# An attention and feed-forward kernel on one core: the list schedule's durations, its transfers, its buffers and its order made anew

## The chip, the core and the metric

The kernel runs on one core of one Trainium2 chip. The metric is the device time of one execution in microseconds (us). A core has five engines with an instruction queue each, and each works through its queue in order: PE (TensorE, matrix products; its weight loads are shown apart as PEld), DVE (VectorE), ACT (ScalarE), POOL (GpSimd) and SP (SyncE), which here only issues transfers (DMAs). An engine that waits for a semaphore holds up all that stands behind the waiting instruction in its queue.

## What is computed

Attention over 8 sequences of 576 positions with 8 heads of 64, a causal window of 128 and a linear bias; its output is the input of a feed-forward layer of 2048 hidden units without biases. All of it is float32.

```python
# attention: q, k, v are [8, 8, 576, 64]
scores = scale * np.matmul(q, k.transpose(0, 1, 3, 2))
mask = (rel >= 0) & (rel < window)                     # rel = row - column, window = 128
scores = np.where(mask, scores + bias[None], -1000000000.0)
attn = np.exp(scores - np.max(scores, axis=-1, keepdims=True))
attn = attn / (np.sum(attn, axis=-1, keepdims=True) + 1e-09)
x = np.matmul(attn, v)                                 # then [4608, 512]
# feed-forward: w_in [512, 2048], w_out [2048, 512]
h = x @ w_in
g = h * erf(np.maximum(h, 0.0) + np.log1p(np.exp(-np.abs(h))))
out = g @ w_out
```

## The kernel before

**Stages.** The 4608 tokens are cut into 12 chunks of 384 (`CH`). A unit of attention is one chunk and one pair of heads, 48 units u in all, four to a chunk. For each of a unit's three tiles PE computes the scores s (L408, float32), DVE adds the bias and finds the row's extreme (L415, two instructions and two short reads of the accumulator), ACT takes the exponential in place in p (L425), DVE inverts the sums (L438 and L439), POOL scales p (L448). PE then transposes p into t (L466), ACT or DVE copies t to pT (L348 or L350), PE multiplies by v into px (L499), and px is split into a rounded part (a copy by ACT or DVE, L348 or L350) and a remainder (DVE, L509), both in the chunk's tile x. Every feed-forward product is made of three float32r products of such parts.

**Two passes.** The first pass (`first_pass`) computes the hidden units of the first 6 of 16 weight blocks as soon as a chunk's x is there: h (L706, per chunk and block two groups of six matmuls of 384 columns), a copy to hs, softplus and erf on ACT in batches (L737 to L740, with table loads), a product and a split on DVE and ACT (L748, L689 or L691, L753), and the products o with w_out (L769, 512 columns). Its partial sums go to DRAM (`pd`, L783). Each x is saved to DRAM as well (`xd`, L681). The second pass (`second_pass`) does the other ten blocks on pairs of chunks with fewer products (`pair`: the tiles pa, pb, pc, L908; copies of pa by `snap` at L689 or L691, sums by `add` at L919), then the same activation (L949, L951) and the products po, pxt, ps, pt (L979); the partial sums are added at L791 and stored at L796. Its weights are prepared in small portions while attention runs (`spare_pair`, `spare_out`: loads `wri` and `wro` at L533, DVE and ACT instructions at L541 to L595, stores `wd` at L600 and L629) and fetched back later.

**What sets the order.** No queue is written by hand. All instructions are registered with `Plan.op`, with an estimated duration on each engine that could take them, the tiles they read and write, and a due time `at`. `Plan.run` (L155) is a list scheduler: it steps through an imagined time, and on each engine starts the ready operation with the lowest due time whose tiles find a free place (`fits`, L198); an operation that ACT or DVE can do goes to the one that is free. The order in which operations start there is the order in which they are emitted into the queues. Durations (`dve`, `act`, `fp32_us`, `f32r_us`, `dma`, L273 to L290), the delay from an engine to the next (`hop`), the moment when a tile's place comes free and the landing of transfers are guesses: on the chip each queue keeps the planned order, but instructions wait for what they really depend on.

**Places.** Tiles live in rings whose sizes are the constants at the top: `NKB` places for q and k, `NQ` for v, `PB` for p, `TB` for pT, `XB` (4) for x, `MB` (18) for the hidden tiles, two each for the staging tiles of weights. PSUM has one bank each for s, t and px and two for h and the second pass' pa, pb, pc. In the first `SPARE` units the scores also use the h banks and the transposes also an o bank. In the first `SINGLE` units each tile's sums are inverted alone, later three together. `NSV` chunks hold their saves of x back until the chunk's last h (L684 and L710). 40 short products on a zero tile (`warm_up`, L343) have the latest due time and fill PE where nothing else is ready.

```python
if c < NSV:
    self.held.setdefault(c, []).append(o)
```

## Time and profile before

| | |
|---|---|
| median of 3 runs | 1035.49 us (1035.35 to 1036.95) |
| the profiled execution's own time | 1035.51 us |
| its span, from the first to the last instruction | 1033.5 us |
| PE busy in the span | 1015.7 us (98%) |
| DVE, ACT, POOL busy | 659.5, 639.8, 161.1 us |
| mean granted TensorE clock | 0.998 |
| moved by DMA | 190.98 MB |

A profile's row names the line, the engine, the operation and the tiles (out<-in, buffer numbers left out), then how often it occurs; a group's row gives the busy time in us, the mean of one in ns, and the idle time of the engine just before it with what ended it. A row of the timeline has the start and the length in us and, in square brackets, the idle time before it and what ended it. A matmul's end is modelled: of matmuls in a row the starts tell the pace, not the lengths.

### The profile page before, as it was taken

The numbers are of one execution on the slowest core, as the hardware profiler recorded it, in microseconds if no ns is written. First come the engines' busy times: TensorE is split into PE (matmuls) and PEld (weight loads), VectorE is DVE, ScalarE is ACT, GpSimd is POOL, SyncE is SP. The second block draws the span as 40 slices with busy tenths as digits, with TensorE's granted clock in tenths as the row PEclk, the third lists the DMA queues.
The fourth block names the chain that finished last, engine by engine and source line by source line (L and its number), as shares of the span: only waits on it lengthen the run. The fifth ranks groups of instructions, "written<-read, shape, count | busy, mean of one in ns | idle before, by whom it ended". The sixth has DMA issues, their size and how long they took to land.

```text
span 1033.5 us, 16056 instructions
## 1 busy us (share of the span) xinstructions
PE 1015.7 (98%) x5612; PEld 927.4 (90%) x5612; DVE 659.5 (64%) x1565; ACT 639.8 (62%) x1283; POOL 161.1 (16%) x294
## 2 busy tenths in 40 slices
PE   9899999989999999999999999999999999999998
PEld 8799998988899899998999998998998988989986
DVE  5888886867788868455347456556566566565532
ACT  5678775766677777666557655645545546548460
POOL 2634234323432213411000000000000000000000
PEclk9999999999999999999999999999999999999999
DMA  9775468689779785563787423324324314310302
GB/s 366 277 250 190 140 205 307 229 287 306 266 297 337 249 300 191 195 226 130 274 326 260 147 96 129 113 87 135 115 75 140 122 66 149 123 62 31 119 4 72
DMA packets 63760, 190.98 MB, mean 185 GB/s; under 512 B 7104, under 2 KB 7872, under 8 KB 63680
## 3 DMA queue, kind: packets, MB, share of 16 engines
q1 hardware_dynamic: 62992, 189.43, 53.1%
q8 instruction: 45, 0.74, 0.3%
q10 hardware_dynamic: 688, 0.52, 0.2%
q14 instruction: 35, 0.29, 0.1%
HBM read 137.76 MB, written 52.17 MB: 184 GB/s over the span
## 4 chain that ended last, share of the span: by engine, by line
PE 87%; DMA 8%; DVE 2%; ACT 1%; issue 1%; POOL 1%; SPq 0%; POOLq 0%; DVEq 0%; ACTq 0%
PE o L769 12%; PE h L706 12%; PE pa L908 12%; PE po L979 12%; PE px L499 8%; PE s L408 7%; PE pc L908 6%; PE pt L979 4%; PE ps L979 4%; PE pxt L979 4%; PE t L466 3%; PE pb L908 3%; DMA xd<-x 2%; DMA qk<-qk_a 1%; DMA wri<-w_in 1%
## 5 line engine op out<-in xcount | busy, mean ns | idle before, releaser
L448 POOL TENSOR_SCALAR p<-p,st 128x192 f32<-128x192 f32 (+1 forms) x288 | 160.4, 575 | 310.5 <-DVE st L439 187.7
L706 PE MATMUL h<-x,wi 128*128 128x384 f32 x864 | 178.3, 347 | 0.5 <-DVE st L438 0.5
L706 PEld LDWEIGHTS h<-x,wi 128*128 128x128 f32 x864 | 150.1, 188 | 3.6 <-PE s L408 0.8
L769 PE MATMUL o<-wo,gh 128*128 128x512 f32 x432 | 144.3, 415 | 0.0
L425 ACT ACTIVATE p<-p,st 128x192 f32<-128x192 f32 (+1 forms) x288 | 124.7, 436 | 19.9 <-DVE st L415 19.6
L689 ACT COPY hs<-pa 128x384 f32<-128x384 f32 x82 | 39.2, 478 | 133.0 <-PE pa L908 132.9
L408 PE MATMUL s<-qk 128*128 128x192 f32 (+1 forms) x576 | 111.5, 318 | 3.9 <-DVE st L415 2.9
L908 PE MATMUL pa<-t,p 128*128 128x384 f32 x540 | 109.3, 337 | 0.2 <-DVE hs L691 0.2
L499 PE MATMUL px<-pT,v 128*128 128x192 f32 (+2 forms) x704 | 105.4, 298 | 2.4 <-DVE x L509 2.0
L499 PEld LDWEIGHTS px<-pT,v 128*128 128x128 f32 x704 | 102.1, 193 | 6.0 <-DVE x L509 2.9
L908 PEld LDWEIGHTS pa<-t,p 128*128 128x128 f32 x540 | 96.4, 188 | 6.4 <-DVE hs L691 0.6
L408 PEld LDWEIGHTS s<-qk 128*128 128x128 f32 x576 | 90.7, 191 | 8.1 <-DVE st L415 2.2
L979 PE MATMUL po<-ho,gh 128*128 128x512 f32 x270 | 90.7, 390 | 0.0
L689 ACT CAST gh<-hs 128x768 fp32r<-128x768 f32 x66 | 55.0, 837 | 56.0 <-DVE hs L959 49.7
L415 DVE CUSTOM_DVE_ANT_0 p<-s,bias 128x192 f32<-128x192 f32 x224 | 70.9, 354 | 26.9 <-PE s L408 20.1
L769 PE MATMUL o<-wo,gl 128*128 128x512 f32 x216 | 85.4, 395 | 0.0
L769 PEld LDWEIGHTS o<-wo,gh 128*128 128x128 f32 x432 | 76.2, 189 | 7.7
L466 PE MATMUL t<-ident,p 128*128 128x128 f32 x400 | 67.7, 275 | 5.6 <-POOL p L448 3.1
L979 PE MATMUL po<-ho,gl 128*128 128x512 f32 x180 | 70.8, 394 | 0.0
L348 ACT COPY pT<-t 128x384 f32<-128x384 f32 (+1 forms) x81 | 36.5, 454 | 49.8 <-PE t L466 45.6
L466 PEld LDWEIGHTS t<-ident,p 128*128 128x128 f32 x400 | 49.6, 144 | 19.1 <-POOL p L448 7.1
L959 DVE TENSOR_TENSOR hs<-s,hs 128x768 f32<-128x768 f32 x60 | 55.4, 952 | 17.0 <-ACT s L951 17.0
(276 smaller groups left out, 1830.0 us busy)
## 6 DMA issues: line engine op xcount, KB each, us to landing
qk<-qk_a SPq DMA_DIRECT2D x31, 768.0 KB, 5.9
xd<-x SPq DMA_DIRECT2D x24, 768.0 KB, 7.1
qk<-qk_c SPq DMA_DIRECT2D x16, 960.0 KB, 6.2
v<-v_a SPq DMA_DIRECT2D x32, 384.0 KB, 5.0
v<-v_c SPq DMA_DIRECT2D x16, 640.0 KB, 4.8
pd<-ot SPq DMA_DIRECT2D x36, 256.0 KB, 4.9
out<-pd SPq DMA_DIRECT2D x36, 256.0 KB, 3.0
p<-wd SPq DMA_DIRECT2D x35, 256.0 KB, 5.1
```

The source lines that it names most:

```text
L408: nc.tensor.matmul(ps[:, j, :n], lhsT=q(t, j), rhs=k(j, off, n), start=True, stop=True)
L415: nc.vector.tensor_tensor_reduce(out=pt[:, c0:, j, :], in0=ps[:, j, :n].rearrange("p (c d) -> p c d", d=D), in1=self.bias[g][:, j, 0::3] i ...
L425: nc.scalar.activation(dst, dst, AF.Exp, bias=low[t][:, j : j + 1], scale=-1.0, accum_out=sums[t][:, j : j + 1])
L448: nc.gpsimd.tensor_scalar(dst, dst, sums[t][:, j : j + 1], 1.0, op0=ALU.mult, op1=ALU.mult)
L466: nc.tensor.matmul(two[:, :, (2 - cb) * D : (3 - cb) * D], lhsT=p[t][:, cb].rearrange("p j d -> p (j d)"), rhs=self.ident[:, :], is_transp ...
L499: nc.tensor.matmul(px[:, to : to + m * D], lhsT=v[:, blk].rearrange("p j d -> p (j d)"), rhs=run(src, m, 256)[:, :, :D], start=first and x ...
L689: self.nc.scalar.copy(out, src)
L706: nc.tensor.matmul(ps[:, :CH], lhsT=ww[:, cs], rhs=xx[:, k], start=(k2 + k + n == 0), stop=(k2 + k + n == 4),)
L769: nc.tensor.matmul(po.all, lhsT=g[:, j, cs], rhs=w.all, start=(u["start"] and n == 0), stop=(u["end"] and n == 2),)
L908: nc.tensor.matmul(dst[:, :CH], lhsT=wv[i](k), rhs=xb[l][:, k], start=start and k + n == 0, stop=k + n == 3, skip_group_check=not start)
L959: op({"DVE": dve(2 * CH)}, lambda e, s=s, hs=hs: V.tensor_tensor(hs.all, s.all, hs.all, ALU.mult), r=[s, *parts], w=parts, at=at)
L979: nc.tensor.matmul(po.all, lhsT=g[:, k, cs], rhs=w.all, start=start and n == 0, stop=end and n == 2)
```

## The change

The scheduler's guesses are replaced. (1) Durations: the fixed part of a VectorE operation falls from 0.14 to 0.047 us, that of a ScalarE one from 0.17 to 0.088 (0.053 out of PSUM), a GpSimd scaling's from 0.49 to 0.24; short float32 matmuls are given twice the time they had. (2) Transfers: before, transfers run one after the other in the plan and an issue behind eight in flight is made longer; now those in flight share the bandwidth by the sizes of their packets (`land`), with 1.3 us (loads) or 0.9 us (stores) after the data, and with eight in flight SP does not issue another one. (3) A tile's place is free in the plan only some 0.1 to 0.2 us after its last user's end (`rest`), and `hop` adds a `tail` for some operations. (4) A GpSimd operation does not start in the plan while a VectorE operation marked `port` runs; GpSimd is asked before VectorE. (5) Constants: `NQ` 3 to 2, `PB` 6 to 9, `TB` 2 to 3, `KH` 4 to 2, `SPARE` 6 to 5, `SINGLE` 2 to 4, `NSV` 5 to 2; the due times of attention (`TE`, `NE`), of the activation (`MC`), of the second pass' products (`MP` 24 to 16) and of the weights (`W1R`; `WS`, `WSD`: the portions of the second pass' weights begin at 110 instead of 140 and are 19 instead of 11 apart). No computation changes; line numbers in the changed kernel are 48 higher from `Attention` on.

```diff
...
-SPARE = 6
-SINGLE = 2
+SPARE = 5
+SINGLE = 4
 WARM = 40
 
-MB, KH, KS = 18, 4, 3
-NQ, NKB, PB, XB, OB, TB = 3, 2, 6, 4, 5, 2
-
-TE, NE = 5.0, 6
+MB, KH, KS = 18, 2, 3
+NQ, NKB, PB, XB, OB, TB = 2, 2, 9, 4, 5, 3
+
+TE, NE = 4.5, 10
 TA = 6.5
-LL, LN, LT = 22, 0.3, 1
+LL, LN, LT = 22, 1, 1
 LEAD = 45
...
-MC, MP, MH = 4, 24, -16
+MC, MP, MH = 0.01, 16, -16
...
-WS, WSD, NWH = 140, 11, 2
-W1R, NSV, GSV = 12, 5, 5
+WS, WSD, NWH = 110, 19, 2
+W1R, NSV, GSV = 8, 2, 5
...
-    def hop(self, src, dst):
+    def hop(self, o, dst):
+        src = o.engine
         if src == "PE":
-            return 0.0 if "PE" in dst else 0.2
-        return 0.2 if "Pool" in dst else 0.14
+            return 0.0 if "PE" in dst else 0.21
+        if o.moved:
+            return 0.14
+        return o.tail + (0.12 if src == "Pool" else 0.28 if "Pool" in dst else 0.15)
 
     def __init__(self):
         self.ops = []
         self.slots = {}
 
-    def op(self, costs, emit, r=(), w=(), at=0.0, moved=0, rows=1.0, count=0):
+    def op(self, costs, emit, r=(), w=(), at=0.0, moved=0, packet=0.0, after=0.0, rows=1.0, count=0, tail=0.0, port=False):
         o = Op()
-        o.count = count
+        o.count, o.tail, o.packet, o.after, o.port, o.landed = count, tail, packet, after, port, False
...
-        transfer, flight = 0.0, []
+        flows, queued, issued, shared = [], [], [], 0.0
+        clock = 0.0
+        used = []
...
+        def land(t):
+
+            nonlocal clock
+            while True:
+                begin = queued[0][0] if queued else 1e9
+                whole = sum(f[1] for f in flows)
+                least = min(flows, key=lambda f: f[0] / f[1]) if flows else None
+                end = clock + least[0] * whole / least[1] if flows else 1e9
+                to = min(begin, end, t)
+                for f in flows:
+                    f[0] -= (to - clock) * f[1] / whole
+                clock = to
+                if end <= to + 1e-9:
+                    flows.remove(least)
+                    o = least[2]
+                    o.lag = clock + o.after - o.end
+                    heapq.heappush(done, (clock + o.after, o.seq, o))
+                    heapq.heappush(events, clock + o.after)
+                elif begin <= to + 1e-9:
+                    o = queued.pop(0)[1]
+                    flows.append([o.moved, o.packet * o.count, o])
+                else:
+                    break
+            nxt = min(begin, end)
+            if nxt < 1e9:
+                heapq.heappush(events, nxt)
+
+        def rest(o):
+            return o.tail + {"PE": 0.21, "SP": 0.14, "Pool": 0.12}.get(o.engine, 0.15)
+
         def fits(o):
+            if o.count and not all(x.landed for x in issued[: max(0, len(issued) + o.count - 8)]):
+                return False
...
-            while done and done[0][0] <= t + 1e-9:
-                _, _, o = heapq.heappop(done)
+            land(t)
+            while used and used[0][0] <= t + 1e-9:
+                _, _, o = heapq.heappop(used)
                 for b in o.bufs:
                     b.users -= 1
                     if b.users == 0 and b.tag is not None:
                         empty[key(b)].append(b.slot)
+            while done and done[0][0] <= t + 1e-9:
+                _, _, o = heapq.heappop(done)
+                o.landed = True
+                while issued and issued[0].landed:
+                    issued.pop(0)
+                over = o.end + o.lag + rest(o)
+                heapq.heappush(used, (over, o.seq, o))
+                heapq.heappush(events, over)
                 for x in o.outs:
                     x.left -= 1
                     if not x.left:
                         late = max(
-                            d.end + d.lag + (self.hop(d.engine, x.costs))
+                            d.end + d.lag + (self.hop(d, x.costs))
                             for d in x.deps
                         )
                         enable(x, max(late, t))
@@ -231,11 +277,13 @@
                 for o in ready[e]:
                     if o.ready > t + self.WAIT[e] + 1e-9 or (best and (best.at, best.seq) < (o.at, o.seq)):
                         continue
+                    if e == "Pool" and shared > t + 1e-9:
+                        continue
                     if fits(o) and all(t + o.costs[e] <= max(free[x], t) + c for x, c in o.costs.items()):
                         best = o
                 return best
 
-            for e in ("SP", "PE", "Act", "DVE", "Pool"):
+            for e in ("SP", "PE", "Act", "Pool", "DVE"):
                 while free.get(e, 0.0) <= t + 1e-9 and ready.get(e):
...
-                    for _ in range(best.count):
-                        if len(flight) >= 8:
-                            best.end = max(best.end, flight.pop(0) + 0.6)
                     free[e] = best.end
-                    if best.moved:
-                        transfer = max(transfer, best.end + 0.65) + best.moved
-                        best.lag = transfer + 0.9 - best.end
-                        flight += [best.end + best.lag] * best.count
+                    if e == "DVE" and best.port:
+                        shared = best.end
                     order.append(best)
-                    heapq.heappush(done, (best.end + best.lag, best.seq, best))
                     heapq.heappush(events, best.end)
-                    heapq.heappush(events, best.end + best.lag)
+                    if best.count:
+                        issued += [best] * best.count
+                        queued.append((best.end + 0.65, best))
+                        heapq.heappush(events, best.end + 0.65)
+                    else:
+                        heapq.heappush(done, (best.end, best.seq, best))
...
 def f32r_us(n):
-    return max(n * 0.000432 + 0.0096, 0.11)
+    return max(n * 0.000428 + 0.0092, 0.11)
 
 
 def fp32_us(n):
-    return 2 * max(n / 1200.0 + 0.003, 0.056)
+    return 2 * max(n / 1200.0 + 0.003, 0.111)
 
 
 def dve(n, fast=False):
-    return 0.14 + n * (0.00054 if fast else 0.00108)
-
-
-def act(n, aps=0, src=0.17):
-    return src + 0.093 * aps + n * 0.00088
-
-
-def dma(nbytes, n=1, run=1536, eng="SP"):
-    return dict(costs={eng: n * 0.6}, moved=nbytes / run * (9 + 0.04 * run) / 16e3, count=n)
+    return 0.047 + n * (0.00054 if fast else 0.00108)
+
+
+def act(n, aps=0, src=0.088):
+    return src + 0.093 * aps + n * 0.00084
+
+
+def dma(nbytes, n=1, run=1536, eng="SP", out=False):
+    packet = 9 + 0.0367 * run
+    return dict(costs={eng: n * 0.42}, moved=nbytes / run * packet / 16e3 + 0.1 * n * (run > 2048), packet=packet, after=0.9 if out else 1.3, count=n)
...
-            op({"DVE": 2 * (dve(n) + 0.08)}, biased, r=[ps, self.bias[g]], w=[pt, low[t]], at=at)
-            op({"Act": 2 * (act(n, 1) + 0.19)}, exps, r=[pt, low[t]], w=[pt, sums[t]], at=at)
+            op({"DVE": 2 * (0.07 + n * 0.0011)}, biased, r=[ps, self.bias[g]], w=[pt, low[t]], at=at)
+            op({"Act": 2 * (0.285 + n * 0.00082)}, exps, tail=0.1, r=[pt, low[t]], w=[pt, sums[t]], at=at)
...
-                op({"Pool": 2 * (0.49 + (3 - c0) * D * 0.0008)}, scaled, r=[p[t], sums[t]], w=[p[t]], at=at)
+                op({"Pool": 2 * (0.24 + (3 - c0) * D * 0.00086)}, scaled, r=[p[t], sums[t]], w=[p[t]], at=at)
...
-        op({"DVE": dve(CH), "Act": act(CH, src=0.145)},
+        op({"DVE": dve(CH), "Act": act(CH, src=0.053)},
            lambda e: self.copy(e, hi.all, px[:, :CH]), r=[px], w=[hi], at=at + 0.1)
...
         op({"DVE": dve(DM)}, lambda e: V.tensor_tensor(flt(t), flt(t), flt(q), ALU.add),
-           r=[q, t], w=[t], at=at)
+           r=[q, t], w=[t], at=at, port=True)
```

The queues move throughout. Three places on PE follow, each first as it stands before, then after the change. Names carry their unit, chunk or block: s4_0 is tile 0 of the scores of unit 4.

The first place is the start of the program, up to the first h. Before:

```order
L408 MATMUL s4_0_593<-qk4_482 128x128 x2
L466 MATMUL t3_2_600<-ident_62,p3_2_524 128x2x64 x3
L499 MATMUL px3_606<-pT3_588,v3_427 128x192
L408 MATMUL s4_1_612<-qk4_482 128x192 x2
L408 MATMUL s4_2_617<-qk4_482 128x192 x2
L499 MATMUL px3_606<-pT3_588,v3_427 128x192 x3
L499 MATMUL px3_606<-pT3_588,v3_427 128x128
L499 MATMUL px3_606<-pT3_588,v3_427 128x64
L408 MATMUL s5_0_639<-qk5_512 128x128 x2
L408 MATMUL s5_1_643<-qk5_512 128x192 x2
L408 MATMUL s5_2_651<-qk5_512 128x192 x2
L706 MATMUL h0_664<-x0_0_429,wi0_497 128x384 x6
```

After:

```order
L547 MATMUL px3_618<-pT3_607,v3_473 128x192 x4
L547 MATMUL px3_618<-pT3_607,v3_473 128x128
L547 MATMUL px3_618<-pT3_607,v3_473 128x64
L456 MATMUL s4_0_636<-qk4_505 128x128 x2
L456 MATMUL s4_1_641<-qk4_505 128x192 x2
L456 MATMUL s4_2_651<-qk4_505 128x192 x2
L456 MATMUL s5_0_659<-qk5_568 128x128 x2
L754 MATMUL h0_667<-x0_0_432,wi0_425 128x384 x6
```

The scores of unit 4, which stood between the transposes and px of unit 3, now follow all of unit 3's work; and the first h stands behind the first tile of unit 5's scores instead of behind all three. Ahead of these rows, 35 of the 40 warm-up products now stand before the first scores, where 7 stood.

The second place is in the first pass: px of units 26, 27 and 28, which read v of the same numbers. Before, from the last matmul of unit 27 to the first of unit 28:

```order
L499 MATMUL px27_3315<-pT27_3245,v27_2899 128x64
L466 MATMUL t28_0_3328<-ident_62,p28_0_3066 128x2x64 x2
L408 MATMUL s30_0_3331<-qk30_3106 128x128 x2
L769 MATMUL o0_24_3337<-wo0_1156,gh24_3143 128x512 x2
L769 MATMUL o0_24_3337<-wo0_1156,gl24_3154 128x512
L466 MATMUL t28_1_3357<-ident_62,p28_1_3094 128x2x64 x3
L769 MATMUL o1_24_3361<-wo0_1156,gh24_3143 128x512 x2
L769 MATMUL o1_24_3361<-wo0_1156,gl24_3154 128x512
L769 MATMUL o2_24_3369<-wo0_1156,gh24_3143 128x512 x2
L769 MATMUL o2_24_3369<-wo0_1156,gl24_3154 128x512
L466 MATMUL t28_2_3380<-ident_62,p28_2_3117 128x2x64 x3
L499 MATMUL px28_3386<-pT28_3341,v28_3250 128x192
```

After, from the last matmul of unit 26 to the first of unit 28, with unit 27 between:

```order
L547 MATMUL px26_3447<-pT26_3030,v26_3023 128x64
L514 MATMUL t28_2_3459<-ident_62,p28_2_3192 128x2x64 x3
L456 MATMUL s31_1_3468<-qk31_3281 128x192 x2
L754 MATMUL h30_3429<-x5_1_2904,wi0_425 128x384 x6
L547 MATMUL px27_3487<-pT27_3154,v27_3398 128x192 x4
L547 MATMUL px27_3487<-pT27_3154,v27_3398 128x128
L547 MATMUL px27_3487<-pT27_3154,v27_3398 128x64
L514 MATMUL t29_0_3503<-ident_62,p29_0_3226 128x2x64 x2
L456 MATMUL s31_2_3509<-qk31_3281 128x192 x2
L817 MATMUL o0_24_3517<-wo0_817,gh24_3338 128x512 x2
L817 MATMUL o0_24_3517<-wo0_817,gl24_3361 128x512
L547 MATMUL px28_3531<-pT28_3401,v28_3463 128x192 x4
```

With two places for v instead of three, v28 takes the place of v26 (before: of v25). After the change seven operations stand between px26 and px28, one of them px27.

The third place is in the second pass, third pair of blocks, fourth pair of chunks: pa is read out by a copy (`snap`, on ACT or DVE) between two groups of products that go to the same bank. Before:

```order
L908 MATMUL pa3_2_8116<-t3_3_7817,p2_4_5847 128x384 x2
L908 MATMUL pa3_2_8116<-t3_3_7817,p2_5_5851 128x384
L979 MATMUL po1_3_8192<-ho6_5728,gh2_8010 128x512
L979 MATMUL po1_3_8192<-lo6_5734,gh2_8010 128x512
L979 MATMUL po1_3_8192<-ho6_5728,gl2_8019 128x512
L979 MATMUL po1_3_8192<-ho7_5746,gh2_8010 128x512
L979 MATMUL po1_3_8192<-lo7_5751,gh2_8010 128x512
L979 MATMUL po1_3_8192<-ho7_5746,gl2_8019 128x512
L908 MATMUL pa3_2_8116<-t4_3_7839,p2_6_5861 128x384 x6
```

After:

```order
L956 MATMUL pa3_2_8141<-t3_3_7830,p2_4_5856 128x384 x2
L956 MATMUL pa3_2_8141<-t3_3_7830,p2_5_5872 128x384
L1027 MATMUL po0_3_8175<-ho7_5743,gh2_8047 128x512
L1027 MATMUL po0_3_8175<-lo7_5751,gh2_8047 128x512
L1027 MATMUL po0_3_8175<-ho7_5743,gl2_8062 128x512
L956 MATMUL pa3_2_8141<-t4_3_7851,p2_6_5884 128x384 x6
```

Between the two groups stood six products of 512 columns, and now stand three. Counted over the second pass, 28 of its 30 pairs have three such products there, where before the least that stood between two groups on the same bank was one group of six products of 384 columns.

More of the change, by code (lines that the diff above doesn't have):

```diff
@@ L439, in inverse @@
                 nc.vector.reciprocal(both(), both())
-            op({"DVE": 0.42}, inverse, r=here, w=here, at=at)
+            op({"DVE": 0.315}, inverse, r=here, w=here, at=at)
             for t in ts:
@@ L740, in tables @@
             A.preload_act_table_set(LOG_EXP_SET)
-        op({"Act": sum(2 * act(p[2]) for p in pairs) + 1.3 * 3}, tables,
+        op({"Act": sum(2 * act(p[2]) + 0.12 for p in pairs) + 1.29 * 3}, tables,
            r=[p[3] for p in pairs], w=[p[4] for p in pairs], at=pairs[0][-1])
```

64 lines of the change are left out of this document (32 added, 32 removed).

## The prediction

> **What bounds the kernel now.** I read the page's head first, then the busy time by stretches, then the list of waits of the stretch in which PE is idle, and last the timeline around each of those waits. The head of the page:
>
> ```profile
> span 1033.5 us, 16056 instructions
> PE 1015.7 (98%) x5612; PEld 927.4 (90%) x5612; DVE 659.5 (64%) x1565; ACT 639.8 (62%) x1283; POOL 161.1 (16%) x294
> ```
>
> PE is busy 98% of the span and no other engine two thirds of it, so PE's own queue sets the time, and the order of the other engines matters only where PE waits. The stretches, with length and PE busy first:
>
> ```profile
> 0.00:60.00 60.00, 53.87 (x349) 51.17 (x350) 43.00 (x169) 37.79 (x132) 24.74 (x48) 0.97 0.82 310
> 60.00:480.00 420.00, 412.63 (x2508) 382.10 (x2507) 315.65 (x982) 301.52 (x776) 136.33 (x246) 1.00 0.72 248
> 480.00:1000.00 520.00, 519.83 (x2631) 470.12 (x2630) 291.73 (x406) 293.72 (x369) 0.00 (x0) 1.00 0.38 128
> ```
>
> There is little to win. From 480 to 1000 us PE stands 0.17 us. From 60 to 480 it stands 420.00 - 412.63 = 7.37 us. In the first 60 us it stands 6.1 us, and the warm-up products count there as busy. Who holds it in the middle stretch, from the list of waits (us in total, times, longest):
>
> ```profile
> ACT x L348 <- DMA xd<-x: 5.5, 2, 3.8
> ...
> DVE wti L544 <- DMA wd<-wto: 3.8, 1, 3.8
> ...
> PE s L408 <- DVE st L415: 2.9, 2, 1.9
> ...
> PE t L466 <- ACT pT L348: 2.2, 3, 1.1
> ...
> PE px L499 <- DVE x L509: 2.0, 2, 1.1
> ...
> ACT wqi L541 <- DMA wri<-w_in: 1.3, 1, 1.3
> ```
>
> PE's seven waits sum to 2.9 + 2.2 + 2.0 = 7.1 us, nearly all of the 7.37. They name DVE and ACT, but those were themselves standing, as the timeline around four of them shows:
>
> ```profile
> 164.98 0.48 ACT L348 CAST x<-px 128x384 fp32r<-128x384 f32 x1 [1.74 <-DMA xd<-x]
> ...
> 165.99 0.30 PE L466 MATMUL t<-ident,p 128*128 128x128 f32 x1 [0.73 <-ACT pT L348]
> ...
> 211.22 0.43 DVE L544 TENSOR_SCALAR wti<-wqi 128x512 int32<-128x512 int32 x1 [3.79 <-DMA wd<-wto]
> ...
> 212.25 0.43 PE L408 MATMUL s<-qk 128*128 128x192 f32 x1 [1.95 <-DVE st L415]
> ...
> 270.40 0.48 ACT L348 CAST x<-px 128x384 fp32r<-128x384 f32 x1 [3.78 <-DMA xd<-x]
> ...
> 270.91 0.56 DVE L509 TENSOR_TENSOR x<-px,x 128x384 fp32r<-128x384 f32 x1 [1.52 <-ACT x L348]
> ...
> 271.52 0.43 PE L499 MATMUL px<-pT,v 128*128 128x192 f32 x1 [1.12 <-DVE x L509]
> ...
> 297.68 0.30 PE L466 MATMUL t<-ident,p 128*128 128x128 f32 x1 [0.35 <-ACT pT L348]
> ```
>
> At 211.22 DVE has stood 3.79 us because it may not overwrite a staging tile of the weights before that tile's store has landed; the reading of the scores stands behind it in DVE's queue, and PE stands 1.95 us for that. So the seven waits sort by the transfer at their root. Saves of x: both px waits and the 0.73 us at 165.99, 2.7 us. Stores of staging tiles: both s waits and the 0.35 us at 297.68, 3.2 us. The load wri: the third t wait, 2.2 - 0.73 - 0.35 = 1.1 us. What the change can take is these 7.1 us and a part of the start.
>
> **The change part by part.** The sum is made against the profiled execution's own time, 1035.5 us, which is the median of the runs; 2.0 us of it lie outside the span. PE's products are the same and as many, and the order of the last 20 us is unchanged, so no term comes from either.
>
> *The start.* The issues of q and k for units 4 and 5 and of v between them, with their landings (KB each, us from issue to landing), and PE from 35 us on:
>
> ```profile
> 25.06 0.33 SPq L368 DMA_DIRECT2D qk<-qk_a  x1
> 26.34 0.33 SPq L380 DMA_DIRECT2D v<-v_a  x1
> 27.61 0.33 SPq L368 DMA_DIRECT2D qk<-qk_a  x1
> ```
>
> ```profile
> qk<-qk_a SPq DMA_DIRECT2D x1, 768.0 KB, 10.4
> ...
> v<-v_a SPq DMA_DIRECT2D x1, 384.0 KB, 10.1
> ...
> qk<-qk_a SPq DMA_DIRECT2D x1, 768.0 KB, 10.8
> ```
>
> ```profile
> 12.35 3.29 PE L343 MATMUL warm_ps<-warm 128*128 128x128 f32 x28
> ...
> 35.56 0.55 PE L466 MATMUL t<-ident,p 128*128 128x128 f32 x3 [1.31 <-POOL p L448]
> 35.94 0.61 PE L408 MATMUL s<-qk 128*128 128x128 f32 x4
> ...
> 36.90 0.49 PE L499 MATMUL px<-pT,v 128*128 128x192 f32 x2
> 37.23 1.46 PE L408 MATMUL s<-qk 128*128 128x192 f32 x8
> 38.53 1.53 PE L499 MATMUL px<-pT,v 128*128 128x192 f32 x10
> 39.90 1.97 PE L408 MATMUL s<-qk 128*128 128x128 f32 x12
> 42.39 0.93 PE L706 MATMUL h<-x,wi 128*128 128x384 f32 x4 [0.52 <-DVE st L438]
> ```
>
> The landings are at 35.5, 36.4 and 38.4 us, and the rest of unit 3 stands behind s of unit 4, so behind the first of them. From the distances, 1.0 us for 384 KB and 2.0 us for 768, a weight load of 512 KB takes 1.3 us. In the new order one such load more stands ahead of unit 4's q and k, and v no longer stands between: landings at 36.8 and 38.8 us. Behind the second come one tile of scores, about 0.5 us, and then h: at 39.3 instead of 42.39 us, 3.1 us earlier. Against it, two tiles of unit 5's scores, eight records at (38.53 - 37.23) / 8 = 0.16 us, now stand behind the first h: 1.3 us. That is **-1.8 us**. The warm-up products that now stand ahead of the first scores make those later; the cover is the loads, for which PE fills 3.3 us with such products at 12.35 us. If that cover is gone, at most these 3.3 us are lost.
>
> *Late transfers.* The save of x that is followed by a new writer of the same place (four places, `XB`) has 4.0 to 4.1 us of PE's work between its issue and that writer in three cases of the old order; in the new one the least are 5.0 and 12.3 us, because from chunk 2 on a save is no longer held to the chunk's last h. Two of three go: -2.2 of the 2.7 us, the rest left to the one at 5.0. For staging stores the order gains little: 17 stores with under 3 us before their overwriting become 14, but the portions are 19 apart instead of 11, so fewer loads are in flight beside them. I take half, -1.6 of 3.2; nothing and all are the ends. Of the 1.1 us for the load, about half, -0.5. Together **-4.3 us**, between -2.2 and -7.1.
>
> On what the plan's new transfers are worth, the landings above bear: they are 1.0 and 2.0 us apart, each by its own size. The Trainium skill, "DMA: Bandwidth & Descriptors", section "Queues, rings and completion order", says that descriptors on each DMA engine are consumed in ring order; by that rule the transfers of SP's queue are served one after the other, and the new plan, in which they share, lets none land later than it counts on. By that rule of the Trainium skill this term would be -7.1 us; by the order's distances it is -4.3.
>
> *Two places for v instead of three.* v of unit u+2 may be loaded only when px of unit u is done, and PE itself waits if it lands late. Between px26 and px28 in the new order stand five transposes (0.38 / 3 = 0.13 us each), eight score records of 0.16 us, px27 (0.33 + 1.37 = 1.70 us), six h and three o. The paces of the last two, and the copy of pa for the next term, are in the second pass, from the timeline:
>
> ```profile
> 994.06 1.20 PE L908 MATMUL pa<-t,p 128*128 128x384 f32 x6
> ...
> 995.10 0.39 PE L979 MATMUL po<-ho,gh 128*128 128x512 f32 x1
> ...
> 995.30 0.48 ACT L689 COPY hs<-pa 128x384 f32<-128x384 f32 x1 [1.25 <-PE pa L908]
> ...
> 995.33 0.40 PE L979 MATMUL po<-lo,gh 128*128 128x512 f32 x1
> ```
>
> ```profile
> 859.25 0.55 DVE L691 COPY hs<-pa 128x384 f32<-128x384 f32 x1
> ...
> 859.86 1.32 PE L908 MATMUL pa<-t,p 128*128 128x384 f32 x6 [0.17 <-DVE hs L691]
> ```
>
> A product of 384 columns takes (995.10 - 994.06) / 6 = 0.173 us, one of 512 columns 0.23 us. So 0.6 + 1.3 + 1.7 + 1.0 + 0.7 = 5.3 us stand between px26 and px28, and v28's issue is written 1.3 us into that, which leaves 4.0 us. Counted in the same way for all units behind the first 30 us, twelve have under 5.8 us: 2.7, 4.0, 4.1, 4.2, 4.3, 4.5, 5.1, 5.2, 5.2, 5.5, 5.6 and 5.7; before, none has under 9. What v takes:
>
> ```profile
> DMA to landing us min/median/max: 2.9/4.8/10.5
> ```
>
> The shortfalls sum to 0 for a landing after 2.7 us or less, 0.2 for 2.9, 1.3 for 4.0, 5.0 for 4.8 and 8.4 for 5.3. The median includes the crowded start, and the close places are those where the plan sees few transfers in flight, so I take 4.0, in the lower half: **+1.3 us**, from +0.2 to +8.4.
>
> *The bank of px.* At eleven places the new order puts the next unit's px 1.55 to 1.77 us behind the last one. Copy to product is 271.52 - 270.40 = 1.12 us, and the copy starts 0.2 us behind the product (as the copy of pa, 995.30 against 995.10), 1.32 in all. It fits where the copying engine is free; for the few where it isn't, **+0.2 us** (0 to 2).
>
> *The second pass.* In 28 of 30 pairs only three products, 3 x 0.23 = 0.69 us, stand between the two groups that use the bank of pa. The turn is 0.20 us to the copy, 0.48 us for it on ACT and 0.06 us to the product (859.86 against 859.25 + 0.55), 0.74 us in all, or 0.81 us on DVE. That is 0.05 to 0.12 us short, 28 times: 1.4 to 3.4 us. I take ACT's, less the 0.17 us of the only wait there now: **+1.2 us**; nothing is the lower end, if the pipelined start of a product hides it. The products with w_out keep 16 us or more behind their activations in either order.
>
> The other constants (`PB`, `TB`, `SINGLE`, `KH`, due times, GpSimd's rule) cost or bring nothing of their own: p, pT and POOL stand behind none of the seven waits, and the two engines that carry the extra copies are busy 302 and 316 of 420 us.
>
> Sum: -1.8 - 4.3 + 1.3 + 0.2 + 1.2 = -3.4 us, **1032.1 us**.
>
> **The rivals.** *All waits go*: the plan's transfers are close enough that none of the seven waits is left, v is on time and the copies keep pace: -1.8 - 7.1 - 0.2 = -9.1 us, 1026.4. For it: each wait stems from a transfer, and that is what the new plan counts differently. Against it: 14 staging stores still have under 3 us. The rule of the Trainium skill named above leads here. *No change*: the staging stores and the load are late as before, only the saves of x go: -1.8 - 2.2 + 1.3 + 0.2 + 1.2 = -1.3 us, 1034.2. For it: 17 close stores against 14. *Slower by v*: with v landing after 5.3 us, PE stands at the twelve units for 8.4 us: -1.8 - 4.3 + 8.4 + 0.2 + 1.2 = +3.7 us, 1039.2. It turns into a loss when the shortfall exceeds 4.7 us, at a landing of about 4.75, near the median of 4.8; against it, that median includes the crowded start.
>
> **How the numbers follow.** A measurement of this kernel can tell 0.2%, about 2.1 us, from no change. My forecast gets 0.38, all waits gone 0.20, no change 0.20, slower by v 0.22. The forecast's own range is 1030 to 1034, by half the bounds of the terms. The range of 1026.4 to 1039.2 reaches from one outer rival to the other; beyond lie the start's 3.3 us and more. Faster by over 0.2% (under 1033.4): the first two and a little of the third, less the upper edge of the first, 0.57. Within: 0.21. Slower: 0.22.
>
> **What would show it.** In the changed kernel's profile the first h should start near 39.3 us; the ACT and DVE waits for a save of x should be gone and those for staging stores halved; PE's idle time from 60 to 480 us should be about 4.5 us, of it 1.3 us as px waiting for v; and from 480 to 1000 us some 1.4 us should be pa waiting for hs, 0.05 us a time. Twelve waits of px for v of 0.5 us or more would make the forecast wrong to the slow side, no wait at all in the middle to the fast side. A first h behind 42 us would refute the start's term.

## The result, and the profile after

The changed kernel takes 1047.87 us (median of 4 runs, 1046.9 to 1050.44) against 1035.42 us for the kernel before: 1.0122 times as long, with a 95% interval of 1.0099 to 1.0144. The forecast was 1032.1 us, and the range ended at 1039.2. The page's head and the stretches, as they were shown of before (length, then busy time of PE, its weight loads, DVE, ACT and POOL, the clock, DMA share and GB/s):

```profile
span 1047.0 us, 16036 instructions
PE 1024.4 (98%) x5612; PEld 924.4 (88%) x5612; DVE 653.1 (62%) x1568; ACT 650.5 (62%) x1288; POOL 167.6 (16%) x294
```

```profile
0.00:60.00 60.00, 50.60 (x316) 45.64 (x317) 45.52 (x173) 36.80 (x124) 21.96 (x42) 0.97 0.77 278
60.00:480.00 420.00, 411.71 (x2488) 377.28 (x2487) 312.32 (x995) 289.08 (x759) 145.64 (x252) 1.00 0.70 244
480.00:1000.00 520.00, 519.10 (x2611) 464.94 (x2611) 279.22 (x380) 306.67 (x387) 0.00 (x0) 1.00 0.39 134
```

PE's idle time grew by little: 9.4 us in the first 60 us (6.1 before), 8.3 to 480 us (7.4), 0.9 to 1000 us (0.2). That is 5 us of the 13.5 by which the span grew. The rest hides in "busy", which is 1024.4 instead of 1015.7 us for the same 5612 products: the end of a matmul is modelled, and a product whose successor starts late can count as busy until then. So the starts have to be read. For the table below, each product is given the distance to the next start that it usually shows when it runs in a row (0.227 us for 512 columns, 0.173 for 384, 0.162, 0.109 and 0.056 for the float32 records of 192, 128 and 64). The **delay** is the start of a product less the work ahead of it at these paces. All profiles of the table have the same work, 982 us with the warm-up products, so delays at the same work compare, whatever the order. Each row is one execution (e12's is the slowest of its four, 1034.47 us), and a lower granted clock counts as delay too (from 20 to 40 us it was 0.91 before, 0.95 after and 0.79 in e5). In us:

| work done | 30 | 60 | 100 | 160 | 480 | 981 |
|---|---|---|---|---|---|---|
| before | 13.4 | 14.3 | 16.4 | 19.7 | 40.7 | 47.1 |
| after | 17.0 | 20.8 | 24.7 | 29.8 | 50.1 | 60.7 |
| e4, serial transfers | 13.8 | 19.3 | 24.8 | 30.2 | 51.0 | 61.9 |
| e5, changed planner, old constants | 20.9 | 27.3 | 32.9 | 36.0 | 58.5 | 67.8 |
| e6, old planner, new constants | 12.5 | 18.9 | 21.7 | 23.5 | 42.1 | 47.5 |
| e7, old durations | 12.9 | 21.9 | 24.0 | 25.3 | 38.0 | 46.5 |
| e9, old DVE durations | 13.7 | 18.2 | 20.9 | 22.8 | 38.8 | 49.0 |
| e12, old durations and serial | 12.8 | 17.8 | 20.0 | 21.3 | 39.5 | 45.8 |
| e13, weights' DVE alone | 14.6 | 18.2 | 20.7 | 28.6 | 52.0 | 61.5 |
| e14, the other DVE alone | 17.1 | 21.0 | 23.5 | 25.5 | 44.0 | 54.2 |

The 13.6 us between before and after come in three pieces: 6.5 us by 60 us of work, 3.6 more by 160, and 4.2 in the second pass (from 480 on, 9.4 to 13.6). Between 160 and 480 us of work the changed kernel is 0.7 us better.

PE's waits of the changed kernel, the largest first:

```profile
PE t L514 <- POOL p L496: 7.6, 12, 1.2
PE px L547 <- ACT pT L396: 1.9, 3, 1.0
PE t L514 <- DVE pT L398: 1.6, 3, 1.2
```

Neither v nor a save of x is in the whole list; the waits of the transposes for POOL are 7.6 us, where the kernel before has 3.1 in its whole list. The start, from the timeline of PE and of SP's queue:

```profile
10.62 0.39 PE L391 MATMUL warm_ps<-warm 128*128 128x128 f32 x2
10.85 0.61 PE L456 MATMUL s<-qk 128*128 128x128 f32 x4
...
16.14 0.33 PE L514 MATMUL t<-ident,p 128*128 128x128 f32 x1 [0.21 <-POOL p L496]
```

```profile
9.25 0.43 SPq L581 DMA_DIRECT2D wro<-w_out  x1
14.24 0.33 SPq L416 DMA_DIRECT2D qk<-qk_a  x1
```

```profile
44.40 0.39 PE L456 MATMUL s<-qk 128*128 128x128 f32 x2
44.70 0.58 PE L754 MATMUL h<-x,wi 128*128 128x384 f32 x2
```

The first scores start behind the warm-up products at 10.85 us instead of 4.20; SP's queue stands from 9.7 to 14.24 us for the place that they free; the first h starts at 44.70 instead of 42.39 us. Last, the stretch from 60 to 160 us, of before and then of after:

```profile
60.00:160.00 100.00, 99.93 (x627) 94.12 (x626) 85.19 (x258) 78.41 (x198) 34.76 (x60) 1.00 0.57 187
```

```profile
60.00:160.00 100.00, 97.64 (x616) 90.19 (x615) 92.30 (x291) 74.14 (x205) 42.46 (x70) 1.00 0.78 277
```

DVE is busy 92 instead of 85 us of 100, and ACT 74 instead of 78. Which of DVE's work came forward shows in its groups over the first 160 us, the same step of preparing weights before and after:

```profile
L546 DVE SCALAR_TENSOR_TENSOR wti<-wqi,wti 128x512 int32<-128x512 int32 x8 | 5.8, 725 | 0.0
...
L546 DVE SCALAR_TENSOR_TENSOR wto<-wqo,wto 128x512 int32<-128x512 int32 x6 | 4.1, 679 | 0.0
```

```profile
L594 DVE SCALAR_TENSOR_TENSOR wti<-wqi,wti 128x512 int32<-128x512 int32 x10 | 7.0, 695 | 0.0
...
L594 DVE SCALAR_TENSOR_TENSOR wto<-wqo,wto 128x512 int32<-128x512 int32 x8 | 5.5, 681 | 0.0
```

18 weight tiles have passed this step instead of 14, and both kernels have passed 32 by 480 us.

### The profile page after: what moved, and what is told of

Its sections match the earlier page's. It is cut to its first block, busy times and chain, and to the rows that moved or that the text cites. A ratio compares the mean times of both kernels' runs of the same rounds, so it can differ in the third digit from the quotient of the medians.

```text
span 1047.0 us, 16036 instructions
## 1 busy us (share of the span) xinstructions
PE 1024.4 (98%) x5612; PEld 924.4 (88%) x5612; DVE 653.1 (62%) x1568; ACT 650.5 (62%) x1288; POOL 167.6 (16%) x294
## 4 chain that ended last, share of the span: by engine, by line
PE 78%; DVE 12%; DMA 4%; issue 3%; POOL 2%; ACT 0%; POOLq 0%; DVEq 0%; SPq 0%
PE pa L956 12%; PE po L1027 12%; PE o L817 10%; PE h L754 9%; PE px L547 6%; PE pc L956 6%; PE s L456 5%; PE pt L1027 4%; PE pxt L1027 4%; PE ps L1027 4%; PE t L514 3%; PE pb L956 3%; DVE p L463 3%; POOL p L496 2%; DMA wd<-wto 1%
## 5 line engine op out<-in xcount | busy, mean ns | idle before, releaser
L496 POOL TENSOR_SCALAR p<-p,st 128x192 f32<-128x192 f32 (+1 forms) x288 | 166.9, 598 | 306.1 <-DVE st L487 211.4
L956 PE MATMUL pa<-t,p 128*128 128x384 f32 x540 | 112.0, 342 | 0.9 <-DVE hs L739 0.9
L737 ACT CAST gh<-hs 128x768 fp32r<-128x768 f32 x74 | 61.5, 838 | 79.6 <-DVE hs L1007 75.2
L737 ACT COPY hs<-pa 128x384 f32<-128x384 f32 x90 | 43.2, 480 | 108.2 <-PE pa L956 108.1
L956 PEld LDWEIGHTS pa<-t,p 128*128 128x128 f32 x540 | 93.8, 188 | 10.6 <-ACT hs L737 8.7
L456 PEld LDWEIGHTS s<-qk 128*128 128x128 f32 x576 | 89.2, 190 | 13.7 <-issue 5.4
L739 DVE COPY hs<-pa 128x384 f32<-128x384 f32 x30 | 16.7, 557 | 92.6 <-PE pa L956 92.6
L967 DVE TENSOR_TENSOR hs<-pc,hs 128x384 f32<-128x384 f32 x60 | 33.4, 556 | 64.4 <-PE pc L956 38.4
```

Of the source, the lines that this page charges most:

```text
L456: nc.tensor.matmul(ps[:, j, :n], lhsT=q(t, j), rhs=k(j, off, n), start=True, stop=True)
L496: nc.gpsimd.tensor_scalar(dst, dst, sums[t][:, j : j + 1], 1.0, op0=ALU.mult, op1=ALU.mult)
L737: self.nc.scalar.copy(out, src)
L956: nc.tensor.matmul(dst[:, :CH], lhsT=wv[i](k), rhs=xb[l][:, k], start=start and k + n == 0, stop=k + n == 3, skip_group_check=not start)
```

## The experiments

Each kernel ran beside the kernel before on the same chip, but not all on one chip, so the ratios are what compares; after's is 1.0122. Since 0.1% is 1.0 us, differences of ratios are given in us too. No experiment changes what is computed.

**e1: fewer warm-up products.**

```diff
-WARM = 40
+WARM = 8
```

> The changed kernel with 8 warm-up products instead of 40, all still ahead of the first scores. Theory (the start is lost because 35 warm-up products stand ahead of the first scores, and each later step waits for the one before): the first scores start near 4.7 us instead of 10.85, the bias lands at 8.6 us and holds the first DVE step to 8.7 instead of 11.61, so everything up to the first h comes about 2.9 us earlier: first h near 41.8 us, time near 1045.0 us (1044 to 1046). Rival (the loads hold the start: q and k of unit 4 land at 38.4 us whatever the scores do): first h stays at 44 to 45 us, time 1047 to 1048.5 us. Second rival (the warm-up products hold up the granted clock): the clock of the first 60 us falls below 0.97 and the time is 1048 us or more.

1050.55 us, 1.0147 (1.0122 to 1.0172): no gain. The stretches of 20 us from the start:

```profile
0.00:20.00 20.00, 12.60 (x52) 9.91 (x53) 7.21 (x40) 10.86 (x37) 4.59 (x15) 0.77 0.93 357
20.00:40.00 20.00, 15.87 (x76) 13.16 (x76) 18.39 (x66) 11.26 (x37) 8.57 (x15) 0.80 0.88 336
```

The scores start at 4.37 us and the first transpose at 12.81 instead of 16.14, as the theory says, but the granted clock is 0.77 and 0.80 where the changed kernel has 0.97 and 0.95, the first h starts at 47.73 us, and what was won is lost again. The second rival holds: the warm-up products pay for the clock. This run can't say what their place costs.

**e2: a dearer copy of pa in the plan.**

```diff
         def snap(src, dst):
-            op({"Act": act(CH, src=0.053), "DVE": dve(CH)}, ...
+            op({"Act": act(CH, src=0.203), "DVE": dve(CH) + 0.15}, ...
```

> The changed kernel, where the plan alone counts 0.15 us more for the copy of pa in the second pass, so that six products of 512 columns stand between the two groups of products on pa's bank instead of three. Theory (at 28 places the turn of pa costs 0.05 us at the group's first product and 0.11 us at its second, because the weight load waits too): 28 x 0.16 = 4.5 us less, time near 1043.5 us (1043 to 1045). Rival (0.05 us a place, as forecast): 1.4 us less, 1046.5 us. Second rival (the second pass is longer for another reason): 1047 to 1048.5 us.

1043.44 us, 1.0079 (1.005 to 1.0108): 4.5 us less than after, as the theory said. One of the 28 places in the changed kernel, the weight loads' row and the products':

```profile
985.41 0.48 ACT L737 COPY hs<-pa 128x384 f32<-128x384 f32 x1 [2.32 <-PE pa L956]
...
985.68 0.40 PE L1027 MATMUL po<-ho,gl 128*128 128x512 f32 x1
...
985.94 0.19 PEld L956 LDWEIGHTS pa<-t,p 128*128 128x128 f32 x1 [0.31 <-ACT hs L737]
985.95 0.45 PE L956 MATMUL pa<-t,p 128*128 128x384 f32 x1
```

```profile
986.23 0.52 PE L956 MATMUL pa<-t,p 128*128 128x384 f32 x2
```

The wait stands at the weight load, not at the product. The first product starts 0.27 us behind the last po (0.227 in a row), and the second 0.28 us behind the first (0.173): its own weight load had no time to run ahead. That is 0.05 + 0.11 us. In the changed kernel's list of waits of weight loads, and then in e2's, where six products stand between, the same wait:

```profile
PEld pa L956 <- ACT hs L737: 8.7, 28, 0.3
```

```profile
PEld pa L956 <- DVE hs L739: 0.4, 1, 0.4
```

**e3: GpSimd's old duration.**

```diff
-op({"Pool": 2 * (0.24 + (3 - c0) * D * 0.00086)}, scaled, ...
+op({"Pool": 2 * (0.49 + (3 - c0) * D * 0.0008)}, scaled, ...
```

> The changed kernel with the old duration of GpSimd's scaling in the plan (0.49 instead of 0.24 us as its fixed part, so 0.64 instead of 0.41 us for 192 columns; the profile of the changed kernel has 0.60). Theory (the plan puts the transposes too close behind a scaling that VectorE stretches): the 12 waits of t for POOL, 7.6 us, fall to 3 us or less, time 1042 to 1045 us. Rival (GpSimd is late because DVE, which it waits for, is late, and the loss of the first pass comes from transfers and copies): the waits only change their name, time 1046.5 to 1049 us.

1052.05 us, 1.0164 (1.014 to 1.0188), slower still. PE's waits:

```profile
PE t L514 <- DVE pT L398: 4.2, 5, 1.7
PE s L456 <- DVE st L463: 3.6, 5, 1.9
PE t L514 <- POOL p L496: 3.1, 6, 0.9
```

The waits for POOL fell from 7.6 to 3.1 us, and those for DVE took their place (1.6 to 4.2, 1.1 to 3.6). My theory falls, and the rival's mechanism holds, though the time is above its 1046.5 to 1049 us too: POOL was only the last to be late.

**e4: transfers one after the other in the plan.**

```diff
-                whole = sum(f[1] for f in flows)
-                least = min(flows, key=lambda f: f[0] / f[1]) if flows else None
-                end = clock + least[0] * whole / least[1] if flows else 1e9
+                least = flows[0] if flows else None
+                end = clock + least[0] if flows else 1e9
...
-                for f in flows:
-                    f[0] -= (to - clock) * f[1] / whole
+                if flows:
+                    least[0] -= to - clock
```

> The changed kernel, where transfers run one after the other in the plan again, with the changed kernel's durations, delays and limit of eight in flight. Theory (sharing the bandwidth lets the first transfers land late in the plan, so the scores are put behind the warm-up products, and transfers on the chip land in the order of issue): the first scores start near 4.7 us, first h by 41 us, and fewer late transfers afterwards, time 1041 to 1045 us. Rival (the model of the transfers matters little beside durations and constants): first h at 43 us or later, time 1046.5 to 1049 us.

1052.12 us, 1.0165 (1.0129 to 1.0201), above the ranges of both. The first scores start at 4.62 us and the first h at 41.51, so the sharing model did put the scores behind the warm-up products. In the table the first 30 us of work are won back (13.8, against 17.0 after and 13.4 before). That this is the price of the scores' place is not shown, since the edit moves the whole order: e7 and e9, below, lose as little in the first 30 us of work (12.9 and 13.7) with their first scores at 11.79 and 10.44 us, still behind the warm-up products. From there to 160 us the delay grows by 16.4 us (12.8 after, 6.3 before): the larger loss is elsewhere.

**e5, e6, e7: the planner or the constants, and which part of the planner.** e5 is the changed planner with all constants of before, e6 the planner of before with all constants of the change, e7 the changed kernel with the old durations of PE, DVE, ACT and POOL. Cut to the core:

```diff
# e5 (e6: the same lines the other way, in the kernel before)
-SPARE = 5
+SPARE = 6
-NQ, NKB, PB, XB, OB, TB = 2, 2, 9, 4, 5, 3
+NQ, NKB, PB, XB, OB, TB = 3, 2, 6, 4, 5, 2
...
# e7
 def dve(n, fast=False):
-    return 0.047 + n * (0.00054 if fast else 0.00108)
+    return 0.14 + n * (0.00054 if fast else 0.00108)
 def act(n, aps=0, src=0.088):
-    return src + 0.093 * aps + n * 0.00084
+    return src + 0.093 * aps + n * 0.00088        # and src=0.17, 0.145 for PSUM
...
```

> The changed planner (durations, transfers, free places, GpSimd's rule) with all constants of before. Theory (the planner's new rules make an order that the chip can't keep in the first 160 us, whatever the constants): delay of the first pass as in the changed kernel, time 1044 to 1050 us. Rival (the constants, such as fewer places for v and earlier weights, cost the time): first pass as before, time 1034 to 1039 us.

> The planner of before with all constants of the change. Theory (the loss is the planner's rules): time 1035 to 1041 us, with the first 160 us within 3 us of before. Rival (the loss is the constants): 1044 us or more, with the first 160 us some 10 us behind before.

> The changed kernel with the durations of before for every operation of PE, DVE, ACT and POOL in the plan; the transfers, the free places, GpSimd's rule and the constants stay as changed. Theory (durations near the shortest traced leave an order without slack, and each engine's queue stands for the next): the first pass wins back most of its loss and six products stand between the groups of pa, time 1036 to 1041 us. Rival (the new transfers or the rule of later free places cost the first pass): first pass as in the changed kernel, 1043 to 1047 us with the second pass' 4.5 us gone.

e5: 1056.42 us, 1.0212 (1.019 to 1.0233). e6: 1035.53 us, 1.0013 (0.9995 to 1.0031). e7: 1033.92 us, 0.999 (0.9976 to 1.0004), 13.7 us less than after. So the constants cost nothing in total that can be told, the new planner loses with either set, and with the new constants the durations are the cause; the new transfers and the later free places are not. Two times missed their theory's range: e5 is slower than 1050 us, e7 faster than 1036. In the table e7's delay grows by 14.0 us from 100 to 480 us of work, where before's grows by 24.3 and after's by 25.4. Of these 10.3 us less than before, e6 has 3.9 by the constants alone (20.4); the other 6.4 come with the rest of the new plan. But e7 is 7.6 us behind before at 60 us of work and e6 4.6, and in both the gain and the loss nearly cancel.

**e8: one term of the forecast alone, in the kernel before.**

```diff
-W1R, NSV, GSV = 12, 5, 5
+W1R, NSV, GSV = 12, 2, 5
```

> The kernel before with NSV = 2 alone: saves of x are held back for two chunks instead of five. Theory (the forecast's term: three saves of x held up ACT or DVE and cost PE 2.7 us): those waits go, time 1032.5 to 1033.5 us. Rival (the transfers that the earlier saves collide with are late in turn, or the order is worse elsewhere): 1035 to 1037 us.

1035.87 us, 1.0009 (0.9991 to 1.0027): no gain. From its list of waits between 60 and 480 us:

```profile
ACT wqo L541 <- DMA wd<-sa: 5.0, 2, 2.6
...
PE t L466 <- ACT pT L348: 4.1, 4, 1.7
...
DVE wh__3975 L592 <- DMA wd<-wh__3907: 3.5, 1, 3.5
...
PE s L408 <- DVE st L415: 2.7, 3, 1.4
```

No wait for a save of x is left, and PE stands no shorter than before (9.9 us in this stretch against 7.4, in a profiled execution of 1039.03 us, above the median): stores of staging tiles are late instead, up to 3.5 us. The rival holds.

**e9, e10, e11: whose slack.** e9 takes back DVE's durations alone, e10 ACT's alone, and e11 leaves all durations and counts 0.1 us more behind every DVE and ACT operation.

```diff
# e9
-    return 0.047 + n * (0.00054 if fast else 0.00108)
+    return 0.14 + n * (0.00054 if fast else 0.00108)
...
# e11
-return o.tail + (0.12 if src == "Pool" else 0.28 if "Pool" in dst else 0.15)
+return o.tail + (0.12 if src == "Pool" else 0.38 if "Pool" in dst else 0.25)
```

> The changed kernel with DVE's durations of before in the plan, all else as changed (three products stay between the groups of pa, so the second pass keeps its loss of some 4.5 us). Theory O (DVE's time is what the plan must not count too short, since DVE is over 90% busy in the first 160 us and everything queues behind it): the first pass wins back most of 10 us, time 1037 to 1041 us. Rival S (any engine's slack will do): 1041 to 1045 us, with ACT's durations and the later hand-over alike. Rival N (neither): 1046 us or more.

> The changed kernel with ACT's durations of before in the plan, all else as changed (six products then stand between the groups of pa, which is worth 4.5 us by itself). Theory O (DVE's time decides): 1043 to 1045 us, the first pass as in the changed kernel. Rival S (slack of any kind): 1037 to 1041 us.

> The changed kernel, where the plan counts 0.1 us more from the end of a DVE or ACT operation to whoever waits for it; durations stay as changed (six products between the groups of pa). Theory O (DVE's occupied time decides, not the delay behind it): 1042 to 1045 us, the first pass as in the changed kernel. Rival S (slack between the engines is what the new plan lacks): 1036 to 1040 us, the waits of t for POOL and of s for DVE halved.

e9: 1038.58 us, 1.0017 (1.0004 to 1.003), 10.9 us less than after, with the turn of pa still in it. e10: 1043.86 us, 1.0067 (1.0052 to 1.0082). e11: 1044.2 us, 1.0073 (1.0054 to 1.0091). These two win 5.7 and 5.1 us, little more than the 4.5 of the turn of pa, which their orders mend. Theory O holds: it is the time that DVE is counted as occupied. (Its premise, DVE over 90% busy in the first 160 us, holds only from 60 us on: 45.5 of the first 60 us, 92.3 of the next 100.) The stretch from 60 to 160 us of e9:

```profile
60.00:160.00 100.00, 97.72 (x610) 90.35 (x609) 81.17 (x259) 77.44 (x211) 38.47 (x66) 1.00 0.71 250
```

DVE is busy 81 us instead of 92. The step at which 18 weight tiles were counted above tells where the difference comes from. By 160 us the tiles past it are:

| tiles | kernels |
|---|---|
| 14 or 15 | before, e6, e7, e8, e9, e12, e15 |
| 16 | e10, e13, e14 |
| 17 or 18 | after, e1, e2, e3, e4, e5, e11 |

e5, with every constant of before, has 18, and e6, with every due time of the change, has 14: the new planner brings the weights forward, not their due times, and within it DVE's durations do (e7 has 14, e9 has 15). That the work brought forward is what holds up attention is not settled by the count: e10 and e14 both have 16, and at 160 us of work e10 is as late as the changed kernel (30.1 against 29.8), e14 is not (25.5).

**e12: old durations with serial transfers.** The edits of e4 and e7 together.

> The changed kernel with the durations of before and with transfers one after the other in the plan. Theory (the old durations keep the first pass, and by the serial transfers the scores come ahead of the warm-up products and the start is no longer lost): first scores at 4.2 to 4.8 us, delay at 60 us of work some 5 us less than with old durations alone, time 1027 to 1031 us, faster than both kernels. Rival (the sharing model was what took the late transfers away between 100 and 480 us): 1034 us or more, with the waits for stores of staging tiles back.

1032.31 us, 0.9952 (0.9936 to 0.9969): 3 to 7 us faster than the kernel before and 17.6 us faster than the changed one. It is above the theory's 1027 to 1031 us. The scores start at 4.20 us. Against e7 it is 4.1 us less behind at 60 us of work, near the 5 expected, but not at 30 (12.8 and 12.9), so the scores' place ahead of the warm-up products is not what wins it. At 160 us of work it is 1.6 us behind before, and it gains 2.8 us from there to 480. Its largest wait names the remainder:

```profile
PE t L513 <- DVE pT L397: 5.2, 2, 4.2
PE t L513 <- POOL p L495: 2.4, 3, 1.0
PE px L546 <- DMA v<-v_a: 2.2, 1, 2.2
```

The 4.2 us are one wait at 190 us, where ACT stands 4.03 us for a load wri, DVE for ACT and PE for DVE.

**e13, e14, e15: which of DVE's work, and do the causes add.** e13 takes the old DVE durations for the preparation of weights alone, e14 for all else alone; e15 joins e9, e4 and e2.

```diff
# e13
+def dve_w(n, fast=False):
+    return 0.14 + n * (0.00054 if fast else 0.00108)
...
-        op({"DVE": dve(DM)}, lambda e: V.tensor_tensor(flt(t), flt(t), flt(q), ALU.add),
+        op({"DVE": dve_w(DM)}, lambda e: V.tensor_tensor(flt(t), flt(t), flt(q), ALU.add),
...
```

> The changed kernel with DVE's old durations for the preparation of weights alone (three products stay between the groups of pa). Theory W (counted short, weights' work is put into DVE's queue ahead of attention's): the first pass wins back most of 10 us, time 1037 to 1041 us, DVE busy under 86 us between 60 and 160 us. Rival A (attention's and feed-forward's own operations, counted short, bring the rest too close behind them): 1045 to 1049 us.

> The changed kernel with DVE's old durations for everything but the preparation of weights (three products stay between the groups of pa). Theory W: 1045 to 1049 us. Rival A: 1037 to 1041 us. Both alike, 1041 to 1045 us, would say that the sum of DVE's queue counts and not its kind.

> The changed kernel with DVE's old durations, transfers one after the other in the plan and 0.15 us more for the copy of pa there. Theory (the three causes are separate and add): 1038.6 less 4.5 for pa and 1 to 5 for the start, 1029 to 1033 us, at least as fast as old durations with serial transfers. Rival (the start's loss is not the warm-up products' place, and late transfers come back with the serial plan): 1034 us or more.

e13: 1049.32 us, 1.0125 (1.0101 to 1.015), no gain. e14: 1042.49 us, 1.0061 (1.0045 to 1.0076), 6.3 us less than after. e15: 1034.69 us, 0.9987 (0.9963 to 1.001). In e13's profile the first 100 us of work are mended as in e9 (delay 20.7, against 20.9 in e9 and 24.7 after), and then single late transfers take it back, of which this is the largest:

```profile
PE px L551 <- DMA v<-v_c: 4.1, 1, 4.1
```

e14 is the opposite: its first 100 us of work stay slow (23.5), and from 100 to 480 it is 4.9 us better than after (20.5 against 25.4). So neither theory alone holds; each part of DVE's work seems to mend its own stretch, but with one profile of each, and with single waits of 4 us in them, the split stays open. e15's causes don't add to what was expected: its runs lie between 1030.98 and 1042.09 us, and its median is above e12's. The time of a run goes with its granted clock, 1.000 in the two fastest and 0.993 in the slowest, which is the profiled one.

## Why the prediction was wrong, point by point

*What bounds the kernel* was right: PE's queue, and waits of PE that stem from in-order DVE and ACT. What the forecast did not ask is how the new durations would change the place of DVE's work, and that was the cause. That is the step that failed: the sum has no term for the new durations and gives no reason for leaving them at nothing. Only the other constants, the due times and GpSimd's rule are argued to "cost or bring nothing of their own", since p, pT and POOL stood behind none of the seven waits, and that too argues from the waits of the old order about an order that all durations make anew. What the runs showed in its place: e9, with DVE's durations of before alone, wins back 10.9 of 12.6 us (1.22% of 1035.4); e3, e10 and e11 show that neither POOL's nor ACT's durations nor the hand-over do. How the durations cost that time is shown in part. In the changed plan DVE's operations are some 0.09 us shorter each, and weights are prepared earlier on it, which the count of tiles shows. That attention's own operations queue behind them, and that PE therefore waits for POOL, ACT and DVE in turn, is read from the profile's groups and waits alone; e13 and e14 did not settle it.

*The start*, -1.8 us: the wrong sign. The first h came at 44.70 instead of 39.3 us, and by 60 us of work 6.5 us were lost. The term took the path from the landings of q and k of units 4 and 5 to their scores and on to h. Issued at 29.61 and 32.60 us, they land at 38.4 and 40.3 us (36.8 and 38.8 in the forecast), but the scores of unit 4 start 3 us after theirs, behind unit 3's px, which waits for the copy of t:

```profile
39.75 1.93 PE L547 MATMUL px<-pT,v 128*128 128x192 f32 x12 [0.50 <-ACT pT L396]
41.52 1.97 PE L456 MATMUL s<-qk 128*128 128x128 f32 x12
```

So it was attention's own chain, not the loads, that ended last there. "The cover is the loads" failed too: the loads wait for places that the scores free, as SP's queue shows at 14.24 us. But the scores' place does not explain the late h, for e9's first h starts at 41.36 us with its scores still behind the warm-up products. Nor is an early h a gain: e6's starts at 39.71 us, as forecast, and e6 is 4.6 us behind before at 60 us of work. There every kernel of the table with the new constants is at least 3.5 us behind, and e5, with the old ones and the changed planner, 13.0. DVE's durations mend 2.6 of the changed kernel's 6.5 us (e9's 18.2 against 20.8); the cause of the remainder stays open. The landings' distances were right: in the changed kernel the first weight loads of 512 KB land 1.27 to 1.29 us apart, by 1.3 in the forecast. This agrees with the Trainium skill, "DMA: Bandwidth & Descriptors", section "Queues, rings and completion order", by which descriptors are consumed in ring order. But that the new plan then lets no transfer be late did not follow: where transfers share in the plan, a short one issued behind a long one lands first, and served in order it lands after it.

*Late transfers*, -4.3 us: the waits for saves of x went as forecast, none is left between 60 and 480 us. Those of DVE and ACT for stores of staging tiles fell there from 15.5 to 10.3 us, not to half. The gain didn't come: 0.7 us between 160 and 480 us of work, and PE stood 8.3 us from 60 to 480 us, not 4.5. e8 shows why for the saves alone: other transfers are late in their place. With the planner of before all the new constants do bring 3.9 us from 100 to 480 us of work (e6), near the term, after losing 5.3 before that. What the new plan adds there with the old durations, 6.4 us in e7, is only 0.9 in e12, without the sharing; one execution of each can't say more.

*Two places for v*, +1.3 us: nothing; no px waits for v in the changed kernel. The slower rival was not what happened, though its mechanism is real: one v is late by 4.1 us in e13 and by 2.2 us in e12.

*The bank of px*, +0.2 us: 0.4 us (px waits once for the remainder of x). *The second pass*, +1.2 us: the mechanism was right and the term mis-sized, 4.2 us by the delay and 4.5 us by e2. The 0.05 us a place were exact; the 0.11 us of the second product's weight load were not in the working, though the page gave weight loads a row of their own.

*The range* was bounded by transfers alone, so its upper end was too low by 8.7 us.

## What to carry to other kernels

When a planner's durations change, the whole order is new: look first at the engine nearest to full, and at what the new order puts ahead of the work that the bound waits for, not at the waits of the old order. The new durations are close to the pace that DVE keeps in a row: a copy of pa is 0.462 us in the plan, and in the changed kernel's trace the next start follows at 0.47 us, while the record itself lasts 0.56. The old plan counted 0.555. The true pace gave the worse order here; that what the plan doesn't model has to fit somewhere is a likely reason, which no run here shows. Give the fullest in-order engine the slack, and test the durations by themselves. A turn of a PSUM bank that was 0.05 us short cost three times that here, as the weight load lost its lead with it.

## What the runs showed of the hardware

- A wait that ends late at a weight load costs the following product too: 0.05 us at the first product and 0.11 at the second, 28 times alike.
- With 16 warm-up records instead of 80 the granted clock of the first 40 us was 0.77 and 0.80 instead of 0.97 and 0.95. The Trainium skill, "TensorE: Matmul & The Clock Gate", section "Part 1: The HAM clock gate", says that the throttled state is the default and activity releases it; e1's rows agree.
- One program's runs can spread over 1%: ten of e15 lie between 1030.98 and 1042.09 us, where thirteen of the kernel before on the same chip lie between 1034.08 and 1038.75. The mean granted clock goes with it, from 1.000 to 0.993; in the profile of the slowest it is 0.91 from 140 to 160 us, where PE is busy 18.07 of 20 us. Which comes first, the wait or the clock, isn't shown, and what makes e15's order so uneven wasn't tried.
